# Preparing the second layer's weights for a fast pass: a second buffer for the high halves, low halves written over the sums, and decoding in four steps

## The chip, the cores and the metric

One core of one Trainium2 chip runs the whole program. The metric is the device time of one execution in microseconds. The kernel before took a median of 1413.3 us over three runs (1409.53, 1413.3 and 1413.33). A separate execution was recorded by the profiler; the rows below come from that one.

## The reference

Three layers follow each other, all in float32. The first is a linear attention with a decaying state for two sequences of 768 tokens; its output x has 1536 tokens of 512 values. The second is a mixture of eight experts whose gates are normalised in turn over experts and tokens. The third is a feed-forward layer with a leaky maximum:

```
for e in range(E):                      # 8 experts, F = 1024
    h = np.maximum(x @ w1[e], 0.0)
    ye = h @ w2[e]
    out += P[:, e:e + 1] * ye
...
h = x @ w_in                            # d_ff = 2048, two halves of 1024
g = np.maximum(h, 0.0) + alpha * np.minimum(h, 0.0)
return (g @ w_out).astype(np.float32)
```

The weights `w_in` and `w_out` arrive as 64-bit floating-point numbers, which the kernel turns into float32 itself.

## The kernel before

Every float32 product is made of three matmuls (`mm3`, lines 186 to 188): each operand is split into a high half (a rounded copy, made by ScalarE) and a low half (what is missing, made by a subtraction on VectorE or GpSimd).

The work runs in 20 phases of one sequence and one expert. Phases 0 to 7 are the eight experts for the first sequence, phases 8 to 15 the same experts for the second, and phases 16 to 19 the two halves of the feed-forward layer. A phase begins with 28 products, each of six matmuls (`product`), in the order of the list `order`: (0,1), (0,5), (0,6), (0,2), (0,7), (1,1), (1,5), (0,4), (1,6), (0,3), (1,2), (1,7), (2,1), (2,5), (1,4), (2,6), and so on; the first number is one of four blocks of the hidden layer, the second one of seven products from which a block is put together. After product (j,1) ScalarE copies bank A to bank B (line 686), and (j,6) adds to B. After (j,6) VectorE writes E from B (line 689), after (j,7) it writes D from B (line 702), and only then may (j,7) and (j,4) respectively add to B again. In phases 0 to 7 and 16 to 19 a second layer follows: six tiles of 128 tokens, each in two halves named t0a, t0, t1a, t1, ... t5a, t5, with 24 matmuls of 512 columns in a half.

In phases 8 to 15 the second layer, too, runs as a product scheme with fewer multiplications. It needs sums of the weights `w2`, which phases 1 to 7 prepare in 32 units. A unit loads a tile `pr` (line 158), forms four sums in it on VectorE (`prep_sums`, line 168), lets ScalarE write the high halves into a tile `pw` (line 170), writes the low halves into the same tile on VectorE (`prep_low`, line 177), and stores the 1 MB of `pw` to memory (`prep_store`, line 183). There is one buffer for `pw` and there are two for `pr`, so ScalarE's write for a unit waits until the store of the unit before it has landed.

The same phases decode the 64-bit weights in 32 steps: three operations on VectorE (`bits`), one on ScalarE (`power`), two more on VectorE (`join`), which also issues the store of 256 KB and the next load.

All this side work hangs on a table of hooks: `at(phase, key, functions)` puts functions behind a product or half tile. The order of the code is the order of each engine's queue, and an instruction that waits holds all that stand behind it on its engine. SyncE issues every transfer from one queue, in order. In phases 1 to 6 a unit's three steps stand at (0,2), (1,1), (1,6); at (2,5), (2,6), (2,7); and at t0a/t0/t1a, t2a/t2/t3a and t4a/t4/t5a. A decoding has all three steps at t1a, t3a and t5a, and stands ahead of the unit's store there.

Of the kernel before, what the change touches and what calls it, by code (L numbers as in the profile page):

```python
# [23 lines left out]
E, F = 8, 1024  # L24
# [5 lines left out]
NJ = NF // 2  # L30
TT = S // 128
# [13 lines left out]
def tile_kernel(ctx, tc, qkT, kv, ctab, w_gate, w1, w2, w_in, w_out, alpha, out):  # L45
    nc = tc.nc
# [7 lines left out]
    pools = {"raw1": stg}  # L54
# [19 lines left out]
    raw = {}  # L74
# [45 lines left out]
    def w1_part(n, part, eng):  # L120
        if n >= NJ * len(PHASES):
            return
        if part == "a":
            ws1[n] = {}
            if n < NJ * E:
                nc.sync.dma_start(out=c1[n], in_=raw[0, n][:, 768:1792])
# [27 lines left out]
    def prep_load(i):  # L154
        if i >= NJ * E:
            return
        pr[i] = tmp.tile([128, 1024], F32, tag=("ua", "ub")[i % 2], name=f"pr{i}")
        nc.sync.dma_start(out=pr[i], in_=w2[i])

    def prep_sums(i):  # L160
        s11, s21, s12, s22 = (pr[i][:, 256 * q:256 * q + 256] for q in range(4))
        for out, in0, in1, op in (
            (s22, s21, s22, ALU.add),
            (s21, s11, s21, ALU.subtract),
            (s11, s22, s11, ALU.subtract),
            (s12, s12, s11, ALU.subtract),
        ):
            nc.vector.tensor_tensor(out=out, in0=in0, in1=in1, op=op)  # L168
        ph2[i] = pools["prep"].tile([128, 4, 2, 256], F32R, tag="pw", name=f"pw{i}")
        nc.scalar.activation(  # L170
            out=ph2[i][:, :, 0, :], in_=pr[i].rearrange("p (a b) -> p a b", a=4), func=AF.Copy
        )

    def prep_low(i):
        v = pr[i].rearrange("p (a b) -> p a b", a=4)
        for a in (0, 2):
            nc.vector.tensor_tensor(  # L177
                out=ph2[i][:, a:a + 2, 1, :], in0=v[:, a:a + 2], in1=ph2[i][:, a:a + 2, 0, :].bitcast(F32),
                op=ALU.subtract,
            )  # L180

    def prep_store(i):
        nc.sync.dma_start(out=c2[i // NJ][:, i % NJ, 3:7], in_=ph2[i].bitcast(F32))

    def mm3(ps, ah, alo, bh, bl, first, last):
        nc.tensor.matmul(ps, ah, bh, start=first, stop=False, skip_group_check=True)  # L186
# [95 lines left out]
    with tc.manual_schedule():  # L282
# [293 lines left out]
        def decode_steps(u, then):  # L576
            kind, j, half = u
            held = {}

            def bits():  # L580
                t = held["t"] = rd.pop(u)
                lo, hi = (t.rearrange("p (f w) -> p f w", w=2)[:, :, q] for q in range(2))
                ex = held["ex"] = tp.tile([128, 512], U32, tag="tmp", name=f"ex{kind}_{j}_{half}")
                nc.vector.tensor_scalar(out=ex, in0=hi, scalar1=0x7FF00000, scalar2=None, op0=ALU.bitwise_and)  # L584
                a = held["a"] = tp.tile([128, 512], U32, tag="tmp", name=f"a{kind}_{j}_{half}")
                nc.vector.tensor_scalar(
                    out=a, in0=hi, scalar1=0x000FFFFF, scalar2=0x00100000, op0=ALU.bitwise_and, op1=ALU.bitwise_or
                )
                nc.vector.scalar_tensor_tensor(
                    out=a.bitcast(F32), in0=lo, scalar=2.0 ** -32, in1=a, op0=ALU.mult, op1=ALU.add  # L590
                )

            def power():
                nc.scalar.activation(out=held["ex"], in_=held["ex"], func=AF.Relu, bias=ebias, scale=8.0)  # L594

            def join():
                t, a, ex = (held[q] for q in ("t", "a", "ex"))
                hi = t.rearrange("p (f w) -> p f w", w=2)[:, :, 1]
                q = a.bitcast(F32)
                nc.vector.scalar_tensor_tensor(  # L600
                    out=q, in0=q, scalar=2.0 ** -20, in1=ex.bitcast(F32), op0=ALU.mult, op1=ALU.mult
                )
# [3 lines left out]
                nc.sync.dma_start(out=wd[kind][j][:, 512 * half:512 * half + 512], in_=q)  # L606
                if then:
                    decode_load(then)

            return bits, power, join  # L610


        banks, hq, late = {}, {}, []
# [268 lines left out]
        def at(ph, key, *fns):  # L882
            hooks.setdefault((ph, key), []).extend(fns)
# [18 lines left out]
        def prep_at(ph, k1, k2, k3):  # L902
            i = unit[0]
            if i >= NJ * E:
                return
            unit[0] += 1
            at(ph, k1, lambda: prep_load(i + 1), lambda: prep_sums(i))
            at(ph, k2, lambda: prep_low(i))
            at(ph, k3, lambda: prep_store(i))

        xk = []
        for ph in range(len(PHASES)):
# [23 lines left out]
                    at(ph, k1, lambda m=m: w1_adds(m, dve), lambda m=m: w1_part(m, "a", dve))  # L936
                    at(ph, k2, lambda m=m: w1_part(m, "c", dve), lambda m=m: w1_part(m, "b", dve))
            if 1 <= ph <= 6:
                for t in (1, 3, 5):
                    decode_at(ph, f"t{t}a", f"t{t}a", f"t{t}a")  # L940
                prep_at(ph, (0, 2), (1, 1), (1, 6))
                prep_at(ph, (2, 5), (2, 6), (2, 7))
                for t in (0, 2, 4):
                    prep_at(ph, f"t{t}a", f"t{t}", f"t{t + 1}a")
            elif ph == 7:
                prep_at(ph, (0, 2), (1, 1), (1, 6))
                prep_at(ph, (2, 5), (2, 6), (2, 7))
            elif fast:
                for q in ((6, 8, 9), (13, 15, 16)) if ph == E else ((4, 6, 7), (12, 14, 15)):
                    decode_at(ph, *(order[i] for i in q))  # L950
                if ph > E + 1:
                    for q in range(8):
                        at(ph, ((0, 5), (0, 7), (1, 5), (1, 6))[q // 2], lambda m=q // 2, h=q % 2: gather(m, h))
                at(ph, (0, 1), lambda ph=ph: weight_load(ph))
                for key, fn, jp in (
                    ((2, 2), t1, 0), ((3, 1), t2, 0), ((3, 6), t3, 0), ((3, 4), t1, 1), (1, t2, 1), (3, t3, 1),
                ):
                    at(ph, key, lambda ph=ph, fn=fn, jp=jp: fn(ph, jp))
                for k, key in enumerate(
                    ((1, 7), (3, 7), (2, 7), 0, (2, 4), 2, 4, 6, 8, 10, 12, 14, 16, 18)  # L960
                ):
                    at(ph, key, lambda ph=ph, k=k: hsplit(ph, k))
                for key, jp in ((5, 0), (7, 1)):
                    at(ph, key, lambda ph=ph, jp=jp: t4(ph, jp))
                if ph in (E + 1, E + 4):
                    at(ph, (0, 1), lambda k=(ph - E - 1) // 3: xk.extend(x_keep(2, k)))
                if E < ph < 2 * E - 1:
                    for keys in (((2, 1), (2, 2), (2, 7), (3, 4)), (9, 11, 13, 17), (18, 20, 22, 27)):
                        i = unit[0] - NJ * E
                        if i >= 7 * ((ph - E - 1) // 3 + 1):  # L970
                            continue
                        unit[0] += 1
                        for q, key in enumerate(keys):
                            at(ph, key, lambda i=i, q=q: xk[i][q]())
# [16 lines left out]
        for a, (key, later) in enumerate(zip(("t3", "t4", "t4", "t5"), (order[i] for i in (0, 1, 20, 22)))):  # L991
# [125 lines left out]
```

## Time and profile before

| quantity | value |
|---|---|
| median of three runs | 1413.3 us |
| profiled execution, its own time | 1405.09 us |
| profiled execution, span | 1403.4 us |
| TensorE busy | 1309.8 us (93%) |
| VectorE busy | 944.8 us (67%) |
| ScalarE busy | 633.9 us (45%) |
| GpSimd busy | 410.3 us (29%) |
| DMA engines, transfers of the hardware queue | 62.6% of their span |
| mean granted TensorE clock | 0.974 |

TensorE is the engine that is nearly always busy. Shares over the whole span hide that the phases differ, so the windows below follow phase boundaries: a phase begins where its first product does (phase 1 at 128.76 us, phase 2 at 197.93, phase 3 at 278.79, phase 7 at 593.09, phase 8 at 673.21). An idle time and its releaser stand in brackets behind the instruction that had to wait. "SPq" is SyncE's queue, "PEclk" the granted clock as a share of full speed.

### The profile page before, as it was taken

What the parts mean: (1) busy time and instruction counts of PE and PEld (TensorE: products, weight loads), DVE (VectorE), ACT (ScalarE), POOL (GpSimd) and SP (SyncE); (2) the same over time, 40 slices, a digit from 0 to 9 for tenths busy, and PEclk for the clock granted to TensorE, in tenths of its full rate; (3) what the DMA queues carried; (4) which work ended last, traced back from release to release, by engine and by line L of the source; (5) the groups of instructions that cost most, each with busy time, mean ns of one, the idle gap of its engine ahead of it and who ended that gap; (6) DMA issues with size and microseconds to landing.
All of it is one profiled execution on the core that took longest, in us unless ns stands there. A gap on an engine that the chain in (4) does not pass through costs nothing.

```text
span 1403.4 us, 19428 instructions
## 1 busy us (share of the span) xinstructions
PE 1309.8 (93%) x7179; PEld 1211.8 (86%) x7179; DVE 944.8 (67%) x1562; ACT 633.9 (45%) x1129; POOL 410.3 (29%) x335
## 2 busy tenths in 40 slices
PE   9899977979797988969999999999999999999998
PEld 6798867868676877868899999999999999889897
DVE  5656676767576676766576887877888576386462
ACT  2543525243332425244445464555645446465460
POOL 4751414131312314131000313123131335336250
PEclk9999999989899999989999999999999999999999
DMA  9563776859586777857776868768676393152201
GB/s 369 175 202 120 245 245 226 297 203 305 204 273 250 252 239 235 292 203 228 240 236 198 291 195 269 241 214 296 185 277 219 123 362 111 44 159 74 85 31 45
DMA packets 123070, 296.79 MB, mean 211 GB/s; under 512 B 11440, under 2 KB 43744, under 8 KB 118880
## 3 DMA queue, kind: packets, MB, share of 16 engines
q1 hardware_dynamic: 122976, 295.56, 62.6%
q8 instruction: 56, 0.92, 0.3%
q14 instruction: 38, 0.31, 0.1%
HBM read 198.24 MB, written 97.28 MB: 211 GB/s over the span
## 4 chain that ended last, share of the span: by engine, by line
PE 62%; DVE 13%; DMA 11%; ACT 6%; issue 4%; SPq 2%; POOL 1%; ACTq 0%; DVEq 0%
PE B L186 7%; DMA c<-pw 7%; PE B L188 7%; PE B L187 7%; PE o L186 5%; PE o L188 5%; PE o L187 5%; PE A L186 4%; PE A L187 4%; PE A L188 4%; DVE pw L177 3%; PE E L188 2%; PE E L186 2%; PE E L187 2%; PE D L188 2%
## 5 line engine op out<-in xcount | busy, mean ns | idle before, releaser
L113 POOL TENSOR_TENSOR raw<-raw 128x256 f32<-128x256 f32 x108 | 94.8, 888 | 234.9 <-DMA raw<-in_w_dram 73.7
L779 DVE TENSOR_TENSOR hs<-b,hs 128x768 fp32r<-128x768 f32 x96 | 97.4, 1015 | 30.9 <-ACT hs L778 30.9
L170 ACT ACTIVATE pw<-pr 128x1024 fp32r<-128x1024 f32 x32 | 33.9, 1059 | 173.7 <-DMA c<-pw 133.5
L778 ACT ACTIVATE hs<-b 128x768 fp32r<-128x768 f32 x96 | 81.1, 844 | 31.0 <-PE B L188 10.7
L811 POOL TENSOR_TENSOR total<-total,t 128x384 f32<-128x384 f32 x56 | 60.0, 1098 | 103.2 <-DVE t L807 103.2
L689 DVE TENSOR_TENSOR E<-B,d 128x384 f32<-128x384 f32 x80 | 45.1, 563 | 58.1 <-PE B L188 53.6
L686 ACT ACTIVATE B<-A 128x384 f32<-128x384 f32 x80 | 38.6, 482 | 87.8 <-PE A L188 86.2
L177 DVE TENSOR_TENSOR pw<-pr,pw 128x512 fp32r<-128x512 f32 x64 | 59.2, 967 | 25.8 <-ACT pw L170 25.8
L250 POOL TENSOR_TENSOR xs<-b,xs 128x384 fp32r<-128x384 f32 x6 | 9.3, 1548 | 193.4 <-ACT xs L246 193.4
L188 PE MATMUL B<-hs,ws 128*128 128x384 f32 x192 | 64.2, 334 | 0.0
L187 PE MATMUL B<-hs,ws 128*128 128x384 f32 x192 | 64.2, 334 | 0.0
L186 PE MATMUL B<-hs,ws 128*128 128x384 f32 x192 | 64.2, 334 | 0.0
L168 DVE TENSOR_TENSOR pr<-pr 128x256 f32<-128x256 f32 x128 | 55.2, 431 | 4.5 <-DMA pr<-in_w_dram 1.2
L594 ACT ACTIVATE ex<-ex,ebias 128x512 uint32<-128x512 uint32 x32 | 23.1, 721 | 63.1 <-DVE ex L584 63.1
L737 DVE SCALAR_TENSOR_TENSOR total<-o,P,total 128x512 f32<-128x512 f32 x42 | 31.3, 746 | 29.6 <-PE o L188 29.6
L702 DVE TENSOR_TENSOR D<-B,d 128x384 f32<-128x384 f32 x48 | 27.1, 565 | 31.4 <-PE B L188 31.0
L186 PE MATMUL A<-hs,ws 128*128 128x384 f32 x128 | 42.9, 335 | 0.0
L187 PE MATMUL A<-hs,ws 128*128 128x384 f32 x128 | 42.9, 335 | 0.0
L188 PE MATMUL A<-hs,ws 128*128 128x384 f32 x128 | 42.8, 335 | 0.0
L731 ACT ACTIVATE total<-o 128x512 f32<-128x512 f32 x18 | 10.8, 598 | 69.0 <-PE o L188 69.0
L113 DVE TENSOR_TENSOR raw<-raw 128x256 f32<-128x256 f32 x84 | 36.9, 457 | 1.4
L645 DVE SCALAR_TENSOR_TENSOR hl<-D,hh 128x384 fp32r<-128x384 f32 x32 | 17.8, 555 | 28.9 <-ACT hh L644 27.2
(3435 smaller groups left out, 4718.0 us busy)
## 6 DMA issues: line engine op xcount, KB each, us to landing
ws<-c SPq DMA_DIRECT2D x112, 512.0 KB, 5.5
raw<-in_w_dram SPq DMA_DIRECT2D x64, 512.0 KB, 4.9
c<-pw SPq DMA_DIRECT2D x32, 1024.0 KB, 6.7
c<-raw SPq DMA_DIRECT2D x32, 512.0 KB, 6.5
pr<-in_w_dram SPq DMA_DIRECT2D x32, 512.0 KB, 6.8
raw<-c SPq DMA_DIRECT2D x32, 512.0 KB, 5.9
raw<-wd SPq DMA_DIRECT2D x32, 512.0 KB, 3.6
raw<-in_w_dram SPq DMA_DIRECT2D x32, 384.0 KB, 4.8
```

The source lines that it names most:

```text
L113: eng.tensor_tensor(out=out, in0=in0, in1=in1, op=op)
L168: nc.vector.tensor_tensor(out=out, in0=in0, in1=in1, op=op)
L170: nc.scalar.activation(out=ph2[i][:, :, 0, :], in_=pr[i].rearrange("p (a b) -> p a b", a=4), func=AF.Copy)
L177: nc.vector.tensor_tensor(out=ph2[i][:, a:a + 2, 1, :], in0=v[:, a:a + 2], in1=ph2[i][:, a:a + 2, 0, :].bitcast(F32), op=ALU.subtract,)
L186: nc.tensor.matmul(ps, ah, bh, start=first, stop=False, skip_group_check=True)
L187: nc.tensor.matmul(ps, ah, bl, start=False, stop=False, skip_group_check=True)
L188: nc.tensor.matmul(ps, alo, bh, start=False, stop=last, skip_group_check=True)
L686: nc.scalar.activation(out=banks[n, "B"], in_=banks[n, "A"], func=AF.Copy)
L689: nc.vector.tensor_tensor(out=banks[n, "E"], in0=banks[n, "B"], in1=banks[n, "d"], op=add)
L778: nc.scalar.activation(out=hi, in_=src, func=AF.Copy)
L779: nc.vector.tensor_tensor(out=lo, in0=src, in1=hi.bitcast(F32), op=ALU.subtract)
L811: nc.gpsimd.tensor_tensor(out=dst, in0=dst, in1=tt[m, h], op=ALU.add)
```

## The change

Four things are edited. The high halves go to a tile `pw` of half the size with two buffers; the low halves are written over the sums in `pr`, which gets a third buffer; the store becomes two stores of 512 KB each, whose pieces in memory are 1 KB long where they were 8 KB. The decoding's store and next load are split off `join` as a fourth step. The hooks move: a decoding's steps spread over several half tiles, one decoding per phase goes into the products, and one unit of the preparation per phase goes from the products to the second layer. The store of the first layer's sums (`c1`) of two blocks per phase goes from part "a" to part "c". The space comes from a smaller scratch area that no transfer of this kernel uses.

```diff
-        pr[i] = tmp.tile([128, 1024], F32, tag=("ua", "ub")[i % 2], name=f"pr{i}")
+        pool = pools["prep"] if i % 3 == 2 else tmp
+        pr[i] = pool.tile([128, 1024], F32, tag="u" + "abc"[i % 3], name=f"pr{i}")
...
-        ph2[i] = pools["prep"].tile([128, 4, 2, 256], F32R, tag="pw", name=f"pw{i}")
-        nc.scalar.activation(
-            out=ph2[i][:, :, 0, :], in_=pr[i].rearrange("p (a b) -> p a b", a=4), func=AF.Copy
-        )
+        ph2[i] = pools["prep"].tile([128, 1024], F32R, tag="pw", bufs=2, name=f"pw{i}")
+        nc.scalar.activation(out=ph2[i], in_=pr[i], func=AF.Copy)
...
-        for a in (0, 2):
+        for a in (slice(0, 512), slice(512, 1024)):
             nc.vector.tensor_tensor(
-                out=ph2[i][:, a:a + 2, 1, :], in0=v[:, a:a + 2], in1=ph2[i][:, a:a + 2, 0, :].bitcast(F32),
-                op=ALU.subtract,
+                out=pr[i][:, a].bitcast(F32R), in0=pr[i][:, a], in1=ph2[i][:, a].bitcast(F32), op=ALU.subtract
             )
...
-        nc.sync.dma_start(out=c2[i // NJ][:, i % NJ, 3:7], in_=ph2[i].bitcast(F32))
+        for q, t in enumerate((ph2[i].bitcast(F32), pr[i])):
+            v = t.rearrange("p (a b) -> p a b", a=4)
+            nc.sync.dma_start(out=c2[i // NJ][:, i % NJ, 3:7, q, :], in_=v)
...
-            return bits, power, join
+            return bits, power, join, store
...
+        slots = [f"t{t}{w}" for t in range(TT) for w in ("a", "")]
...
-            at(ph, k2, lambda: prep_low(i))
+            hooks.setdefault((ph, k2), []).insert(0, lambda: prep_low(i))
...
-                for t in (1, 3, 5):
-                    decode_at(ph, f"t{t}a", f"t{t}a", f"t{t}a")
-                prep_at(ph, (0, 2), (1, 1), (1, 6))
-                prep_at(ph, (2, 5), (2, 6), (2, 7))
-                for t in (0, 2, 4):
-                    prep_at(ph, f"t{t}a", f"t{t}", f"t{t + 1}a")
+                if ph > 1:
+                    decode_at(ph, *(order[i] for i in (10, 12, 14, 18)))
+                for i in (2, 8):
+                    decode_at(ph, *(slots[i + q] for q in (0, 1, 2, (4, 3)[i > 2])))
+                prep_at(ph, order[8], order[10], order[12])
+                for i in (0, 3, 6, 9):
+                    prep_at(ph, *slots[i:i + 3])
```

In `order`, place 8 is (1,6), 10 is (1,2), 12 is (2,1), 14 is (1,4), 18 is (2,7) and 20 is (3,5). Phase 7 gets units at places 8, 10, 12 and 20, 22, 24 and one decoding at 10, 12, 14, 18. In the phases from 8 on the decodings' places move a little and get the fourth step; two transposes move in phase 8.

ScalarE, at the boundary of phases 2 and 3, before. `pw` are the high halves of a unit, `ex` a decoding, `B12` and `d12` the copies that the first products of phase 3 need:

```order
L170 ACTIVATE pw9_2814<-pr9_2715 128x4x256
L594 ACTIVATE ex0_2_1_2844<-ex0_2_1_2844,ebias_78 128x512
L686 ACTIVATE B12_2876<-A12_2869 128x384
L681 ACTIVATE d12_2889<-D12_2882 128x384
L644 ACTIVATE hh12_00_2905<-A12_2869 128x384
L97 ACTIVATE wa14h_2909<-raw0_14_2700 128x512
L170 ACTIVATE pw10_2919<-pr10_2808 128x4x256
L644 ACTIVATE hh12_11_2928<-D12_2882 128x384
```
The same place after the change:

```order
L171 ACTIVATE pw9_2831<-pr9_2758 128x1024
L687 ACTIVATE B12_2875<-A12_2868 128x384
L682 ACTIVATE d12_2888<-D12_2881 128x384
L645 ACTIVATE hh12_00_2904<-A12_2868 128x384
L97 ACTIVATE wa14h_2907<-raw0_14_2690 128x512
L645 ACTIVATE hh12_11_2918<-D12_2881 128x384
```
The decoding step between the last `pw` of phase 2 and the copy `B12` is gone, and so is the `pw` behind `wa14h`.

VectorE in the products of phase 3, from the E addition behind product (1,6) to the D addition behind (1,7), before:

```order
L689 TENSOR_TENSOR E13_2976<-B13_2943,d13_2959 128x384
L645 SCALAR_TENSOR_TENSOR hl12_10_2968<-B12_2876,hh12_10_2967 128x384
L645 SCALAR_TENSOR_TENSOR hl12_01_2987<-E12_2897,hh12_01_2986 128x384
L702 TENSOR_TENSOR D13_2952<-B13_2943,d13_2959 128x384
L645 SCALAR_TENSOR_TENSOR hl13_00_3002<-A13_2936,hh13_00_3001 128x384
```
The same place after:

```order
L690 TENSOR_TENSOR E13_2965<-B13_2934,d13_2948 128x384
L646 SCALAR_TENSOR_TENSOR hl12_10_2957<-B12_2875,hh12_10_2956 128x384
L169 TENSOR_TENSOR pr10_2825<-pr10_2825 128x256 x4
L646 SCALAR_TENSOR_TENSOR hl12_01_2983<-E12_2896,hh12_01_2982 128x384
L175 TENSOR_TENSOR pr10_2825<-pr10_2825,pw10_2974 128x512 x2
L583 TENSOR_SCALAR ex0_2_1_3007<-rd0_2_1_2864 128x512
L585 TENSOR_SCALAR a0_2_1_3009<-rd0_2_1_2864 128x512
L588 SCALAR_TENSOR_TENSOR a0_2_1_3009<-rd0_2_1_2864,a0_2_1_3009 128x512
L703 TENSOR_TENSOR D13_2941<-B13_2934,d13_2948 128x384
```
Between the two additions there now stand the sums (`pr10`) and low halves of a unit and the three operations of a decoding (`ex`, `a`).

SyncE at the end of phase 2's second layer, before. `wd` is the store of a decoding, `rd` the load of the next, `c2` the store of a unit, `raw` and `c1` belong to the first layer:

```order
L606 DMA wd0_2_124<-a0_2_0_2762 128x512
L574 DMA rd0_2_1_2769<-in_w_in_dram 128x1024
L183 DMA c2_2_114<-pw8_2721 128x2048
L91 DMA raw0_15_2793<-in_w1_dram 128x1024
L158 DMA pr10_2808<-in_w2_dram 128x1024
L606 DMA wd0_2_124<-a0_2_1_2846 128x512
L574 DMA rd0_3_0_2853<-in_w_in_dram 128x1024
L183 DMA c2_2_114<-pw9_2814 128x2048
```
The same place after:

```order
L182 DMA c2_2_114<-pw8_2764 128x4x256
L182 DMA c2_2_114<-pr8_2693 128x4x256
L159 DMA pr10_2825<-in_w2_dram 128x1024
L607 DMA wd0_2_124<-a0_2_0_2806 128x512
L573 DMA rd0_2_1_2864<-in_w_in_dram 128x1024
L182 DMA c2_2_114<-pw9_2831 128x4x256
L182 DMA c2_2_114<-pr9_2758 128x4x256
```
Before, each store of a unit stood behind the store of the decoding at its key; now the unit's two stores are ahead of the next decoding's store in one case and still behind one in the other.

## Rows read from the trace of the kernel before

**Rows 1.** Windows, one stretch a row, as its first line names them; (x) counts instructions.
```profile
core 0: us, PE busy (x) PEld busy (x) DVE busy (x) ACT busy (x) POOL busy (x), PEclk, DMA share, GB/s
128.70:197.90 69.20, 64.88 (x316) 58.02 (x316) 49.47 (x84) 31.17 (x54) 20.93 (x16) 0.98 0.72 243
197.90:593.10 395.20, 333.22 (x1562) 298.72 (x1561) 266.07 (x456) 142.20 (x240) 107.19 (x80) 0.93 0.74 250
278.80:357.30 78.50, 66.51 (x313) 59.65 (x312) 53.20 (x92) 28.45 (x48) 21.44 (x16) 0.93 0.74 250
593.10:673.20 80.10, 68.09 (x325) 60.99 (x324) 47.31 (x82) 33.03 (x61) 17.19 (x12) 0.94 0.65 223
1274.70:1337.00 62.30, 62.24 (x313) 56.08 (x312) 32.75 (x59) 31.52 (x57) 24.47 (x18) 1.00 0.23 73
```

**Rows 2.** Waits of TensorE: who waited, for whom, total us, times, longest.
```profile
PE B L186 <- ACT B L686: 53.6, 13, 7.1
```

**Rows 3.** Timeline of TensorE in phase 3: start, us, instruction, idle before and releaser.
```profile
285.80 0.69 PE L186 MATMUL B<-xh,wc12h 128*128 128x384 f32 x1 [4.77 <-ACT B L686]
...
289.00 0.34 PE L187 MATMUL A<-xl,wa12h 128*128 128x384 f32 x1
289.18 0.34 PE L188 MATMUL A<-xh,wa12l 128*128 128x384 f32 x1
...
297.43 0.69 PE L186 MATMUL B<-xh,wc13h 128*128 128x384 f32 x1 [3.75 <-ACT B L686]
...
311.28 0.44 PE L186 MATMUL B<-xh,wc14h 128*128 128x384 f32 x1 [0.87 <-DVE E L689]
...
317.29 0.44 PE L186 MATMUL B<-xh,wb14h 128*128 128x384 f32 x1 [2.60 <-DVE D L702]
```

**Rows 4.** Timeline of ScalarE at the start of phase 3.
```profile
281.84 1.06 ACT L170 ACTIVATE pw<-pr 128x1024 fp32r<-128x1024 f32 x1 [9.10 <-DMA c<-pw]
284.65 0.72 ACT L594 ACTIVATE ex<-ex,ebias 128x512 uint32<-128x512 uint32 x1 [1.76 <-DVE ex L584]
285.28 0.47 ACT L686 ACTIVATE B<-A 128x384 f32<-128x384 f32 x1
```

**Rows 5.** Timeline of SyncE's queue just before phase 3.
```profile
274.05 0.33 SPq L606 DMA_DIRECT2D wd<-a  x1
...
274.94 0.41 SPq L183 DMA_DIRECT2D c<-pw  x1
```

**Rows 6.** Timeline of VectorE in phase 3.
```profile
288.67 1.79 DVE L168 TENSOR_TENSOR pr<-pr 128x256 f32<-128x256 f32 x4
290.59 0.57 DVE L702 TENSOR_TENSOR D<-B,d 128x384 f32<-128x384 f32 x1
...
296.78 2.92 DVE L177 TENSOR_TENSOR pw<-pr,pw 128x512 fp32r<-128x512 f32 x2
...
333.21 1.29 DVE L177 TENSOR_TENSOR pw<-pr,pw 128x512 fp32r<-128x512 f32 x2
334.42 0.42 DVE L584 TENSOR_SCALAR ex<-rd 128x512 uint32<-128x512 uint32 x1
...
335.21 0.69 DVE L589 SCALAR_TENSOR_TENSOR a<-rd,a 128x512 f32<-128x512 uint32 x1
```

**Rows 7.** Timeline of GpSimd beside the row at 296.78.
```profile
297.08 2.07 POOL L98 TENSOR_TENSOR wc14l<-raw,wc14h 128x768 fp32r<-128x768 f32 x1 [5.14 <-ACT wc14h L97]
```

**Rows 8.** Windows: start of the second layer, all of it, the products, five us.
```profile
324.60:335.50 10.90, 10.90 (x50) 9.06 (x49) 7.78 (x18) 2.70 (x4) 1.16 (x1) 1.00 1.01 346
324.60:357.30 32.70, 32.70 (x146) 27.13 (x145) 25.77 (x48) 7.61 (x11) 5.32 (x5) 1.00 0.86 289
278.80:324.60 45.80, 33.81 (x169) 32.52 (x168) 27.43 (x45) 20.84 (x37) 16.12 (x12) 0.89 0.65 222
291.00:296.00 5.00, 2.68 (x16) 2.36 (x14) 0.61 (x2) 1.16 (x2) 0.94 (x1) 0.96 1.00 416
```

More of the change, by code (lines that the diff above doesn't have):

```diff
@@ L122, in w1_part @@
             return
+        if part == "ac"[n % NJ // 2] and n < NJ * E:
+            nc.sync.dma_start(out=c1[n], in_=raw[0, n][:, 768:1792])
         if part == "a":
             ws1[n] = {}
-            if n < NJ * E:
-                nc.sync.dma_start(out=c1[n], in_=raw[0, n][:, 768:1792])
             src, width, pieces = raw[0, n][:, 0:512], 512, (A11, A12)
@@ L168, in prep_sums @@
             nc.vector.tensor_tensor(out=out, in0=in0, in1=in1, op=op)
-        ph2[i] = pools["prep"].tile([128, 4, 2, 256], F32R, tag="pw", name=f"pw{i}")
-        nc.scalar.activation(
-            out=ph2[i][:, :, 0, :], in_=pr[i].rearrange("p (a b) -> p a b", a=4), func=AF.Copy
-        )
+        ph2[i] = pools["prep"].tile([128, 1024], F32R, tag="pw", bufs=2, name=f"pw{i}")
+        nc.scalar.activation(out=ph2[i], in_=pr[i], func=AF.Copy)
     def prep_low(i):
-        v = pr[i].rearrange("p (a b) -> p a b", a=4)
-        for a in (0, 2):
+        for a in (slice(0, 512), slice(512, 1024)):
             nc.vector.tensor_tensor(
-                out=ph2[i][:, a:a + 2, 1, :], in0=v[:, a:a + 2], in1=ph2[i][:, a:a + 2, 0, :].bitcast(F32),
-                op=ALU.subtract,
+                out=pr[i][:, a].bitcast(F32R), in0=pr[i][:, a], in1=ph2[i][:, a].bitcast(F32), op=ALU.subtract
             )
     def prep_store(i):
-        nc.sync.dma_start(out=c2[i // NJ][:, i % NJ, 3:7], in_=ph2[i].bitcast(F32))
+        for q, t in enumerate((ph2[i].bitcast(F32), pr[i])):
+            v = t.rearrange("p (a b) -> p a b", a=4)
+            nc.sync.dma_start(out=c2[i // NJ][:, i % NJ, 3:7, q, :], in_=v)
     def mm3(ps, ah, alo, bh, bl, first, last):
@@ L605, in join, with store @@
                 )
-                nc.sync.dma_start(out=wd[kind][j][:, 512 * half:512 * half + 512], in_=q)
+            def store():
+                nc.sync.dma_start(out=wd[kind][j][:, 512 * half:512 * half + 512], in_=held["a"].bitcast(F32))
                 if then:
                     decode_load(then)
-            return bits, power, join
+            return bits, power, join, store
         banks, hq, late = {}, {}, []
@@ L938, in tile_kernel @@
             if 1 <= ph <= 6:
-                for t in (1, 3, 5):
-                    decode_at(ph, f"t{t}a", f"t{t}a", f"t{t}a")
-                prep_at(ph, (0, 2), (1, 1), (1, 6))
-                prep_at(ph, (2, 5), (2, 6), (2, 7))
-                for t in (0, 2, 4):
-                    prep_at(ph, f"t{t}a", f"t{t}", f"t{t + 1}a")
+                if ph > 1:
[5 more added lines that the diff above has]
+                    prep_at(ph, *slots[i:i + 3])
             elif ph == 7:
-                prep_at(ph, (0, 2), (1, 1), (1, 6))
-                prep_at(ph, (2, 5), (2, 6), (2, 7))
+                decode_at(ph, *(order[i] for i in (10, 12, 14, 18)))
+                prep_at(ph, order[8], order[10], order[12])
+                prep_at(ph, order[20], order[22], order[24])
             elif fast:
-                for q in ((6, 8, 9), (13, 15, 16)) if ph == E else ((4, 6, 7), (12, 14, 15)):
+                for q in ((6, 8, 9, 11), (20, 22, 23, 25)) if ph == E else ((4, 6, 7, 8), (15, 17, 19, 21)):
                     decode_at(ph, *(order[i] for i in q))
@@ L990, in tile_kernel @@
             at(E, ((0, 7), (1, 5), (1, 6), (1, 2), (2, 1), (2, 6))[w], lambda w=w: ws_load(E, w))
-        for a, (key, later) in enumerate(zip(("t3", "t4", "t4", "t5"), (order[i] for i in (0, 1, 20, 22)))):
+        for a, (key, later) in enumerate(zip(("t3", "t4", "t4", "t5"), (order[i] for i in (0, 1, 14, 16)))):
             at(E - 1, key, lambda a=a: turn(2, a, 0))
@@ L1101 @@
     }
-    nc = bacc.Bacc("TRN2", target_bir_lowering=False, num_devices=1, dynamic_dma_scratch_size=1024)
+    nc = bacc.Bacc("TRN2", target_bir_lowering=False, num_devices=1, dynamic_dma_scratch_size=64)
     arrays, args = {}, []
```

## The prediction

> **What bounds the kernel now.** I read the windows by phase first. Phase 18, which prepares nothing, takes 62.3 us, and TensorE is busy in 62.24 of them; phases 2 to 6 take 395.2 us together, 79.0 each, with a granted clock of 0.93 where phase 18 has 1.00 [rows 1]. So some 16.7 us of each of these phases is not matmul work. The loss is not spread evenly. Phase 3 has a second layer of 32.7 us in which TensorE is busy throughout, and products of 45.8 us with 33.81 busy [rows 8]. At full rate the products would take 62.3 - 32.7 = 29.6 us, so the whole loss of 16.2 us stands in the products.
>
> The list of waits names the releaser: TensorE waits 53.6 us in all for ScalarE's copy of A to B [rows 2]. The timeline places it: 4.77 us before product (0,6) and 3.75 before (1,6), then two waits for VectorE, 0.87 and 2.60 [rows 3], together 11.99 us. After the first gap the ten matmuls from 285.80 to 289.00 come 0.32 us apart, while the next pair stands 0.18 apart [rows 3]: TensorE restarts at the lower of its two clock levels (1.2 GHz, not 2.4), which costs 10 x (0.32 - 0.18) = 1.4 us there. The second gap, and what the rounding of these rows hides, leaves 16.2 - 12.0 - 1.4 = 2.8 us, which I take as the same restart after the second gap.
>
> Why is the copy late? ScalarE's `pw` started at 281.84 after 9.10 us of waiting for the store of the unit before, a decoding step came behind it at 284.65, and the copy at 285.28 [rows 4]. That store was issued at 274.94, behind a decoding store at 274.05 [rows 5], and took 281.84 - 274.94 = 6.9 us to land. So the chain is: decoding on VectorE, SyncE's in-order queue, the store, the one `pw` buffer, ScalarE's queue, TensorE.
>
> **What the change removes.** With two buffers a `pw` waits for the store of two units earlier. In the second layer a unit comes every three half tiles, 3 x 32.7 / 12 = 8.2 us. A store follows its `pw` by two half tiles (5.5 us), and the buffer is wanted again 16.4 us after that `pw`: 10.9 us for a store of 6.9. Even with a few us of delay in SyncE's queue this holds. The decoding between the last `pw` and the copy is gone, too, and the second unit in the products, whose sums stood before the E addition and whose low halves stood before the D addition at the waits of 0.87 and 2.60. So all four waits and both restarts go: 16.2 us in phase 3, 16.7 in the mean of five phases.
>
> **What it adds, and what is late next.** Four terms per phase.
>
> First, VectorE's queue in the second layer. It works 25.77 us there now [rows 8]. The change puts in one more set of sums (1.79) and two more sets of low halves that now fall outside (2 x 1.29) [rows 6], while a decoding that ran over into the products goes to the products: 25.8 + 1.8 + 2.6 = 30.1 of 32.7 us. It also waits for ScalarE, since low halves now stand right behind their sums at two of four units and each `pw` takes 1.06 [rows 4], and it starts idle until the first tile is done (half a tile pair, 2.7 us, less the sums that fit in it). I put the end of its queue at 36.5 us from the layer's start. The E addition is wanted three products in, after 32.7 + 4 x 1.05 = 36.9 us, by TensorE's product (0,7); it takes about 0.57 like the D addition [rows 6]. So the wait is between 0 (the queue ends in time) and 3 us (GpSimd holds up VectorE); I take 1.0.
>
> Second, the D addition of block 1. Behind the E addition VectorE now has the sums, 1.79; then a low half of block 0 whose high half stands behind the unit's `pw` on ScalarE, 1.06 + 0.47 of idling; that low half, 0.5; the unit's low halves, 1.29 when free and 2.92 beside GpSimd; and a decoding's three operations, 0.42 + 0.42 + 0.69, or near double [rows 4, 6, 7]. With the E addition done 0.9 us after product (1,6), and one more low half of 0.5, the D addition ends after 0.9 + 0.5 + 1.8 + 1.5 + 0.5 + (1.3 to 2.9) + (1.5 to 2.9) + 0.6 = 8.6 to 11.6 us. TensorE wants it at product (1,4), five products or 5.2 us after (1,6). The wait is 3.4 to 6.4 us; I take 4.4, nearer the lower end, because GpSimd is busy in only 16.12 of 45.8 us of the products [rows 8], though it splits `w1` just there.
>
> Third, a restart at the lower clock after that wait, 1.4 to 2.8 us by the two of before: 2.0. Fourth, the E addition of block 2 follows late, behind a split of `w2` and the decoding's second half: 0 to 1.5, I take 0.5. Sum: 1.0 + 4.4 + 2.0 + 0.5 = 7.9 us, a phase of 62.3 + 7.9 = 70.2.
>
> On the low halves the trace shows 1.29 us for a pair at 333.21 and 2.92 for a pair at 296.78, while GpSimd's split ran from 297.08 to 299.15 [rows 6, 7]: the pair ended about half a microsecond after GpSimd did. The Trainium skill (SBUF — State Buffer, "Who interferes with whom") says that a VectorE tensor_tensor with both inputs in SBUF contends with GpSimd's reads, and that whoever issues second fully blocks. The trace agrees. It speaks against this change, which puts such operations on the way to a D addition; what it does if every one of them is caught is the slower rival below.
>
> The transfers move the same bytes. One more unit's load and store and one decoding less fall in the second layer, where the DMA share is 0.86 of 32.7 us [rows 8]. The 1 KB pieces cost something: in the stretch where the low and high halves of `w2` leave in such pieces, a share of 1.01 moved 346 GB/s, against 416 at 1.00 elsewhere [rows 8]. For 5 MB a phase that is 5243 x (1/346 - 1/416) = 2.5 us of DMA time, hidden unless the engines are full. The Trainium skill (DMA: Bandwidth & Descriptors, "Specifications") gives 512 B as the least transfer at line rate, by which these pieces would cost nothing; the row differs, and I go by the row. The forecast would be the same by either.
>
> **Sum.** Phases 2 to 6: 395.2 - 5 x 70.2 = 44.2 us. Phase 7 takes 80.1 [rows 1] and gains like them, less about 1 for its second unit in the products: 7. Phase 1 (69.2, so 6.9 above phase 18) loses small waits and gets the same sums before a D addition without a decoding: 1.5. The phases from 8 on keep their work: 0, give or take 2. Together 52.7 us, from the profiled 1405.1 to 1352.4. The median shown is 0.6% above the profiled execution and the fastest run 0.3%; between them I forecast 1355 us.
>
> **Rivals.** (A) VectorE keeps up: the D addition comes within the slack of two products, and the phases fall to 63.5. Then phases 2 to 6 give 395.2 - 317.5 = 77.7, phase 7 16, phase 1 5: 1306, some 1310 in the runs. For it: VectorE works 27.43 of 45.8 us in the products now [rows 8], and no row shows the new queue. Against it: the sum of the second term is above its slack at both ends.
>
> (B) The transfers become the bound of the second layer: 0.86 x 32.7 = 28.1 us of DMA time, plus a load and about 1.5 MB of stores at 416 GB/s (2.1 MB in 5.0 us), plus 2.5 for the short pieces, 35.6 against 32.7. Loads of `pr` come late, VectorE waits, and E is late by about 3 us more, with a second restart of about 2: 75 us a phase, a gain of 20 + 4, so 1381. Against it: phases have stretches of 0.65 in their products [rows 8] into which stores can slip.
>
> (C) Slower: GpSimd and VectorE block each other at every step. If each of the two low halves and three decoding operations waits out a GpSimd instruction (2.07 in rows 7, 1.3 for the shorter ones), the second term becomes about 10 us, the first about 6, and with two restarts of 2.8 and the 0.5 the sum is 22: a phase of 84, and 5 x 5 + 5 = 30 us more than before, 1436. It decides from a sum of 16.7 on, which is what is removed. Against it: GpSimd is idle in most of the stretch.
>
> (D) The change doesn't free ScalarE: stores are held in SyncE's queue behind a first-layer store or a decoding store so long that two buffers fill as well, and `pw` still waits: 1405 to 1413.
>
> **How the numbers follow.** Forecast 0.52, A 0.22, B 0.14, C 0.06, D 0.06. A measurement of this kernel tells a change of 0.3%, some 4 us, from none. The forecast, A and B are all faster, and of D a third: 0.90; D gives half of 0.06 to no change, 0.03; C and the rest of D 0.07. The forecast's own range, from its terms at both ends (sums of 4.8 to 13.7), is 1337 to 1382; taking in most of A and B, the range is 1318 to 1390.
>
> **What would show it.** Right: no wait of ScalarE's `pw` for a store, no wait of TensorE for the copy B, one wait per phase of 3 to 6 us before product (1,4) for D, a granted clock near 0.96 in phases 2 to 6. Wrong: no such wait (A), VectorE's sums waiting for `pr` and a DMA share near 1 in the second layer (B), low halves and decoding at twice their time throughout (C), or `pw` still released by a store (D).

## The result, and the profile after

The changed kernel took a median of 1389.6 us (1388.6 to 1390.6, four runs) against 1411.4 of the kernel before on the same chips: a ratio of 0.985 with an interval of 0.982 to 0.988. It is faster by 1.5%, some 22 us, where 58 were forecast (from 1413 to 1355). The time lies just inside the upper end of the stated range, 1318 to 1390. The two executions whose profiles are compared below lie closer together than the medians: their spans are 1403.4 and 1388.9 us, 14.5 apart.

The windows follow the phases again. The first row is phases 2 to 6 together, the second phase 3, then phases 7, 8, and 9 to 15. The columns are those of [rows 1].

```profile
197.64:570.15 372.51, 329.24 (x1562) 295.06 (x1560) 267.89 (x455) 143.24 (x240) 105.76 (x80) 0.94 0.80 265
272.94:347.90 74.96, 66.48 (x314) 59.39 (x313) 54.77 (x93) 29.13 (x49) 21.14 (x16) 0.93 0.81 267
570.15:649.61 79.46, 67.56 (x325) 59.95 (x324) 53.36 (x90) 33.85 (x62) 17.99 (x12) 0.94 0.70 234
649.61:714.66 65.05, 61.91 (x351) 61.13 (x350) 44.28 (x64) 32.86 (x57) 0.00 (x0) 0.97 0.72 234
714.66:1132.90 418.24, 410.18 (x2353) 407.97 (x2353) 319.27 (x438) 220.39 (x376) 94.11 (x83) 1.00 0.71 233
```

Phases 2 to 6 fell from 395.2 to 372.5 us, 74.5 each, where 70.2 were forecast. Phase 7 went only from 80.1 to 79.5. The later phases lost time. Here are phases 8 and 9 to 15 of the kernel before:

```profile
673.20:736.50 63.30, 60.63 (x351) 59.56 (x350) 44.39 (x64) 32.67 (x57) 0.00 (x0) 1.00 0.73 242
736.50:1149.00 412.50, 410.34 (x2353) 407.94 (x2353) 319.30 (x438) 221.48 (x376) 94.97 (x83) 1.00 0.71 236
```

So phase 8 is 1.75 us longer, at a granted clock of 0.97 instead of 1.00, and phases 9 to 15 are 5.7 us longer, 7.5 together. The work of phases 9 to 15 is the same in both: 2353 matmuls and 438 VectorE instructions. What grew there is TensorE's wait for the E addition. In this list for the changed kernel's phases 9 to 15 it is the only wait (the kernel before has 1.5 us of it, and 0.7 for another operation):

```profile
PE B L185 <- DVE E L690: 8.1, 6, 1.6
```

Over the whole execution, TensorE's waits (who waited, for whom, total us, times, longest) answer to [rows 2]:

```profile
PE B L185 <- DVE D L703: 40.3, 8, 5.8
PE B L185 <- ACT B L687: 16.3, 7, 3.8
PE B L185 <- DVE E L690: 13.3, 10, 3.1
```

The wait for the copy B fell from 53.6 to 16.3 us; a wait for the D addition has taken its place. The timeline of TensorE in phase 3 answers to [rows 3]:

```profile
277.57 0.44 PE L185 MATMUL B<-xh,wc12h 128*128 128x384 f32 x1 [2.38 <-ACT B L687]
...
298.01 0.69 PE L185 MATMUL B<-xh,wb13h 128*128 128x384 f32 x1 [5.82 <-DVE D L703]
...
302.65 0.34 PE L187 MATMUL E<-xh,wb13l 128*128 128x384 f32 x1
```

`wb13h` at 298.01 is the product (1,4), the place that the prediction named. The 14 steps from there to the matmul at 302.65 are nearly all 0.32 us long, the lower clock level. They take 4.64 us, against 14 x 0.175 = 2.45 at full rate, so 2.2 us more are lost.

VectorE's and GpSimd's timelines show why D is late. VectorE answers to [rows 6], GpSimd to [rows 7]:

```profile
287.08 0.57 DVE L690 TENSOR_TENSOR E<-B,d 128x384 f32<-128x384 f32 x1 [2.53 <-PE B L187]
...
288.02 2.62 DVE L169 TENSOR_TENSOR pr<-pr 128x256 f32<-128x256 f32 x4
292.19 0.56 DVE L646 SCALAR_TENSOR_TENSOR hl<-E,hh 128x384 fp32r<-128x384 f32 x1 [1.55 <-ACT hh L645]
292.67 2.35 DVE L175 TENSOR_TENSOR pr<-pr,pw 128x512 fp32r<-128x512 f32 x2
294.94 1.48 DVE L583 TENSOR_SCALAR ex<-rd 128x512 uint32<-128x512 uint32 x1
296.34 0.41 DVE L585 TENSOR_SCALAR a<-rd 128x512 uint32<-128x512 uint32 x1
296.79 0.69 DVE L588 SCALAR_TENSOR_TENSOR a<-rd,a 128x512 f32<-128x512 uint32 x1
297.40 0.56 DVE L703 TENSOR_TENSOR D<-B,d 128x384 f32<-128x384 f32 x1
```
```profile
286.57 3.33 POOL L113 TENSOR_TENSOR raw<-raw 128x256 f32<-128x256 f32 x4
292.76 1.72 POOL L98 TENSOR_TENSOR wb14l<-raw,wb14h 128x512 fp32r<-128x512 f32 x1 [2.85 <-ACT wb14h L97]
294.43 1.71 POOL L98 TENSOR_TENSOR wa15l<-raw,wa15h 128x512 fp32r<-128x512 f32 x1
```

The queue is what the order of the change says: sums, idling for the high half behind `pw` (1.55), low halves, three decoding operations, then D at last, which starts 10.3 us after the E addition did. Three of these took longer than in [rows 6]: the sums, which ran beside GpSimd's additions, 2.62 us instead of 1.79; the low halves, beside its two splits, 2.35 instead of 1.29; and the decoding's first operation, beside the second split, 1.48 instead of 0.42.

The wait for the copy B has another cause than before. First VectorE, then ScalarE with the list of what `pw` waits for, then SyncE, with what its queue waited for between 256 and 266 us:

```profile
272.14 0.43 DVE L583 TENSOR_SCALAR ex<-rd 128x512 uint32<-128x512 uint32 x1 [2.63 <-DMA rd<-in_w_in_dram]
```
```profile
ACT pw L171 <- DVE pr L169: 136.0, 30, 8.9
276.09 1.06 ACT L171 ACTIVATE pw<-pr 128x1024 fp32r<-128x1024 f32 x1 [2.70 <-DVE pr L169]
277.05 0.47 ACT L687 ACTIVATE B<-A 128x384 f32<-128x384 f32 x1
```
```profile
SPq L124 <- DVE raw L113: 4.8, 1, 4.8
261.76 0.33 SPq L124 DMA_DIRECT2D c<-raw  x1
262.19 0.38 SPq L182 DMA_DIRECT2D c<-pw  x1
262.62 0.91 SPq L182 DMA_DIRECT2D c<-pr  x1
263.57 1.30 SPq L607 DMA_DIRECT2D wd<-a  x1
264.92 1.19 SPq L573 DMA_DIRECT2D rd<-in_w_in_dram  x1
```

No store of a unit holds `pw` any more, where [rows 4] showed 9.10 us for one. Of its 32 waits 30 are for the sums; the other two, 2.3 and 2.6 us, are put down to a store, but end within 0.1 us of the sums. But the load `rd` for the second layer's second decoding stands in SyncE's queue behind a first-layer store, two stores of a unit and a decoding store. The first of these waited 4.8 us for VectorE's additions and held the others. The load is issued at 264.92, VectorE waits 2.63 us for it, and behind it stand the last unit's sums, its `pw`, and the copy B.

### The profile page after: what moved, and what is told of

It reads as the page before. It is cut to its first block, busy times and chain, and to the rows that moved or that the text cites. A ratio compares the mean times of both kernels' runs of the same rounds, so it can differ in the third digit from the quotient of the medians.

```text
span 1388.9 us, 19473 instructions
## 1 busy us (share of the span) xinstructions
PE 1306.0 (94%) x7179; PEld 1208.2 (87%) x7179; DVE 946.9 (68%) x1562; ACT 634.6 (46%) x1129; POOL 408.6 (29%) x335
## 3 DMA queue, kind: packets, MB, share of 16 engines
q1 hardware_dynamic: 152160, 295.57, 64.2%
## 4 chain that ended last, share of the span: by engine, by line
PE 66%; DVE 18%; ACT 6%; DMA 5%; issue 3%; SPq 2%; POOL 1%; ACTq 0%; DVEq 0%
PE B L185 8%; PE B L187 7%; PE B L186 7%; PE o L185 5%; PE o L187 5%; PE o L186 5%; PE A L185 4%; PE A L187 4%; PE A L186 4%; DVE pr L169 3%; DVE pr L175 3%; PE E L185 2%; PE E L186 2%; PE E L187 2%; PE D L187 2%
## 5 line engine op out<-in xcount | busy, mean ns | idle before, releaser
L113 POOL TENSOR_TENSOR raw<-raw 128x256 f32<-128x256 f32 x108 | 90.1, 845 | 207.3 <-DMA raw<-in_w_dram 62.5
L169 DVE TENSOR_TENSOR pr<-pr 128x256 f32<-128x256 f32 x128 | 65.8, 514 | 3.3
L249 POOL TENSOR_TENSOR xs<-b,xs 128x384 fp32r<-128x384 f32 x6 | 6.1, 1022 | 199.8 <-ACT xs L245 199.8
L187 PE MATMUL B<-hs,ws 128*128 128x384 f32 x192 | 64.2, 334 | 0.0
L185 PE MATMUL B<-hs,ws 128*128 128x384 f32 x192 | 64.2, 334 | 0.0
L186 PE MATMUL B<-hs,ws 128*128 128x384 f32 x192 | 64.2, 334 | 0.0
L175 DVE TENSOR_TENSOR pr<-pr,pw 128x512 fp32r<-128x512 f32 x64 | 48.7, 803 | 16.9 <-ACT pw L171 16.9
L113 DVE TENSOR_TENSOR raw<-raw 128x256 f32<-128x256 f32 x84 | 42.2, 519 | 1.4
L645 ACT ACTIVATE hh<-D 128x384 fp32r<-128x384 f32 x32 | 15.7, 490 | 49.3 <-DVE D L703 49.3
L682 ACT ACTIVATE d<-D 128x384 f32<-128x384 f32 x64 | 31.1, 486 | 15.0 <-PE D L187 14.9
```

What stands on the lines that cost most here:

```text
L113: eng.tensor_tensor(out=out, in0=in0, in1=in1, op=op)
L175: nc.vector.tensor_tensor(out=pr[i][:, a].bitcast(F32R), in0=pr[i][:, a], in1=ph2[i][:, a].bitcast(F32), op=ALU.subtract)
L186: nc.tensor.matmul(ps, ah, bl, start=False, stop=False, skip_group_check=True)
L187: nc.tensor.matmul(ps, alo, bh, start=False, stop=last, skip_group_check=True)
```

## The experiments

The reasons under test: theory Q says the change lost its gain in VectorE's queue, by where it puts the unit and the decoding; theory T says the transfers, in shorter pieces and with late loads, took it. The first four kernels ran on one chip, the other four later on another. Ratios are against the kernel before on the same chip; its medians on the two, 1411.4 and 1413.0 us, differ by 0.1%.

**The storage alone.** The change's two `pw` buffers, three `pr` buffers and two stores, with all hooks (and the store of `c1`) at the places of before.

```diff
-                prep_at(ph, order[8], order[10], order[12])
-                for i in (0, 3, 6, 9):
-                    prep_at(ph, *slots[i:i + 3])
+                for t in (1, 3, 5):
+                    decode_at(ph, f"t{t}a", f"t{t}a", f"t{t}a", f"t{t}a")
+                prep_at(ph, (0, 2), (1, 1), (1, 6))
+                prep_at(ph, (2, 5), (2, 6), (2, 7))
+                for t in (0, 2, 4):
+                    prep_at(ph, f"t{t}a", f"t{t}", f"t{t + 1}a")
...
```

> The storage of the change (two buffers for pw, three for pr, two stores per unit) with the places of the kernel before. Theory Q (VectorE's queue between the E and the D addition, and its late end in the second layer, are what the change lost): the waits for a store go, and no unit with a decoding stands between the E and D addition of block 1; phases 2 to 6 look like phase 1 of the kernel before (69.2 us), 69 to 71 us each, so 1355 to 1370 us, faster than the change by 20 us or more. Rival T (the transfers, with 1 KB pieces and late loads, are what the change lost): phases stay at 74 to 76 us, 1385 to 1395 us.

Measured: 1342.2 us, ratio 0.950 (0.946 to 0.953), better than either theory said. The window is phases 2 to 6:

```profile
197.16:536.07 338.91, 318.46 (x1562) 286.43 (x1560) 273.31 (x456) 143.59 (x241) 105.70 (x80) 0.98 0.88 291
```

That is 67.8 us a phase, with the short pieces and a DMA share of 0.88. One half of theory T falls here: the same short stores at a higher rate (291 GB/s against 265) cost nothing that shows. Its other half, late loads, is not tested by this kernel, since the loads, too, stand at the places of before. The storage is worth 69 us; with it in place, the new places give 47 of them back.

**The places alone.** The storage functions of before in the change.

```diff
-        ph2[i] = pools["prep"].tile([128, 1024], F32R, tag="pw", bufs=2, name=f"pw{i}")
+        ph2[i] = pools["prep"].tile([128, 4, 2, 256], F32R, tag="pw", name=f"pw{i}")
...
```

> The places of the change with the storage of the kernel before (one pw buffer of 1 MB, one store of 8 KB pieces per unit). Both theories: a unit every 8.2 us with a store that is issued 5.5 us after its pw and lands 6.9 us later makes ScalarE wait some 4 us per unit in the second layer; the waits of ScalarE for a store come back, over 80 us in all. Theory Q: the waits for the D addition stay as well, so it is slower than the kernel before, 1415 to 1450 us. Rival T: without the short pieces the loads come in time, so it is between the two, 1390 to 1410 us.

Measured: 1413.2 us, ratio 1.0005 (0.999 to 1.002): no change, a little under Q's interval and above T's. So with the old storage the places cost some 2 us, not clear of noise, against 47 with the new: the effects of storage and places don't add up. ScalarE waits for stores as expected, and TensorE for D as in the change:

```profile
ACT pw L170 <- DMA c<-pw: 119.1, 15, 12.5
```
```profile
PE B L186 <- DVE D L704: 40.3, 8, 5.8
```

The wait for D is 40.3 us with the old storage, too, the same as with the new: it belongs to the places.

**The later phases' places.** The change with the decodings and transposes of phases 8 to 15 where they were.

```diff
-                for q in ((6, 8, 9, 11), (20, 22, 23, 25)) if ph == E else ((4, 6, 7, 8), (15, 17, 19, 21)):
+                for q in ((6, 8, 9, 9), (13, 15, 16, 16)) if ph == E else ((4, 6, 7, 7), (12, 14, 15, 15)):
...
```

> The change with the decodings and transposes of phases 8 to 15 at the places of the kernel before. Theory Q: phases 8 to 15 go back from 483.3 us to 475.8, the waits for the E addition of block 3 there vanish; 1381 to 1384 us. Rival (these phases are slower because of traffic left over from phase 7, or scatter between executions): no change, 1387 to 1391 us.

Measured: 1384.9 us, ratio 0.980 (0.975 to 0.985). Its four executions scatter from 1379.5 to 1391.7 us, so the time alone does not tell this kernel from the change (1388.6 to 1390.6); the phases do. Phases 8 and 9 to 15, and the wait for E in the latter:

```profile
651.15:717.00 65.85, 63.16 (x351) 62.31 (x350) 44.37 (x64) 33.07 (x57) 0.00 (x0) 0.95 0.71 229
717.00:1131.06 414.06, 410.55 (x2354) 407.88 (x2353) 320.00 (x438) 221.25 (x376) 94.95 (x83) 1.00 0.71 236
```
```profile
PE B L185 <- DVE E L690: 2.5, 5, 0.8
```

Phases 9 to 15 get 4.2 of their 5.7 us back, and the wait for E falls from 8.1 to 2.5. The whole set of kernels bears this out: the six with the change's places there take 418.2 to 418.3 us for these phases, the four with the places of before 412.5 to 414.2. Phase 8 gets nothing back, so its 1.75 us are not explained by its decodings and transposes. It has a granted clock of 0.95 here, lower still than the 0.97 of the change.

**The load earlier.** The first decoding of the second layer issues its store and next load with the join, ahead of the first-layer store.

```diff
-                    decode_at(ph, *(slots[i + q] for q in (0, 1, 2, (4, 3)[i > 2])))
+                    decode_at(ph, *(slots[i + q] for q in (0, 1, 2, (2, 3)[i > 2])))
```

> The change with the store and next load of the second layer's first decoding one step earlier, at t2a with the join, ahead of the first layer's store in SyncE's queue. Theory L (the 2.63 us that VectorE waits for the decoding's load at t4a makes the sums and pw of the last unit late, and so the copy B): the wait for the load falls under 0.5 us, the wait of TensorE for the copy falls from some 2.4 us to under 1 in phases 2 to 6, 8 to 14 us less in all, 1375 to 1382 us. Rival W (VectorE has too much work there anyway, 30 of 32.7 us): the copy is as late as before, 1387 to 1391 us.

Measured: 1371.0 us, ratio 0.970 (0.966 to 0.975), a little more than expected; phases 2 to 6 take 71.7 us each. In phase 2 the load now goes out ahead of the first-layer store, and VectorE's operation on it no longer waits:

```profile
254.80 0.43 SPq L573 DMA_DIRECT2D rd<-in_w_in_dram  x1
...
264.74 0.42 DVE L583 TENSOR_SCALAR ex<-rd 128x512 uint32<-128x512 uint32 x1
```

TensorE's list of waits no longer has the copy B; what it has is the D addition, 40.3 us as before, and some more for E:

```profile
PE B L185 <- DVE E L690: 18.3, 14, 3.1
```

So rival W falls, and the late loads of theory T are shown to cost something, by their place in the queue. This one place was worth 19 us: 2.8 us in each of phases 2 to 6, and in phase 7 the 79.5 became 76.0. The next three kernels keep this edit, to take the wait for D apart.

**The decoding behind D.**

```diff
-                    decode_at(ph, *(order[i] for i in (10, 12, 14, 18)))
+                    decode_at(ph, *(order[i] for i in (18, 20, 22, 24)))
```

> As the run with the early load, and the decoding in the products moved from places 10, 12, 14, 18 to 18, 20, 22, 24. Theory Q (the D addition of block 1 is late by just what stands ahead of it on VectorE): the three decoding operations (1.48 + 0.41 + 0.69 less overlaps, 2.5 us) leave the stretch, the wait for D falls from 5.83 to about 3.3 us in phases 2 to 7, each phase gets 2.5 to 4 us shorter, 1348 to 1358 us. Rival (ScalarE's pw and the high half behind it set the D addition, or the decoding costs the same at its new place): the wait stays above 5 us, or the phases stay at 71.7; 1367 to 1374 us.

Measured: 1360.1 us, ratio 0.964 (0.961 to 0.967). The wait in phase 3:

```profile
285.02 0.69 PE L185 MATMUL B<-xh,wb13h 128*128 128x384 f32 x1 [3.36 <-DVE D L703]
```

3.36 for 3.3 expected, and 69.5 us a phase, but 2 us more in all than the range said: phase 7 keeps its decoding there, and with it its wait of 5.83.

**The low halves behind D.**

```diff
-                prep_at(ph, order[8], order[10], order[12])
+                prep_at(ph, order[8], order[12], order[14])
```

> As the run with the early load, and the low halves of the unit in the products moved behind the D addition, from place 10 to 12, with the stores at 14; sums and pw stay. Theory Q: 2.3 us of low halves leave the stretch, the wait for D falls from 5.83 to about 3.5 us, 1350 to 1360 us. Rival: no change, 1367 to 1374 us.

Measured: 1364.0 us, ratio 0.966 (0.964 to 0.968), between the theory's range and the rival's. The wait fell only to 4.5 where 3.5 were expected. TensorE in phase 3, and VectorE, which shows why:

```profile
286.69 0.69 PE L185 MATMUL B<-xh,wb13h 128*128 128x384 f32 x1 [4.51 <-DVE D L703]
```
```profile
282.67 0.42 DVE L583 TENSOR_SCALAR ex<-rd 128x512 uint32<-128x512 uint32 x1
283.00 1.50 DVE L585 TENSOR_SCALAR a<-rd 128x512 uint32<-128x512 uint32 x1
284.53 1.63 DVE L588 SCALAR_TENSOR_TENSOR a<-rd,a 128x512 f32<-128x512 uint32 x1
```

The 2.35 us of low halves went and the first decoding operation is back at 0.42, but now the other two stand beside GpSimd's splits (282.75 to 285.61 us) and take 1.50 and 1.63 instead of 0.41 and 0.69. Whichever operation of VectorE's stands beside the splits is the one that takes longer.

**GpSimd out of the way.** GpSimd's splits of the first layer's weights behind D, in phases 2 to 7.

```diff
+                ka, kc, kb = ((j, 2), (j, 7), (j, 3)) if not 1 < ph < E else ((0, 2), (0, 7), (1, 4)) if j == 0 else ((1, 4), (2, 6), (1, 3))
...
```

> As the run with the early load, and GpSimd's splits of w1 (second part of the third block, all parts of the fourth) moved behind the D addition in phases 2 to 7, so that nothing of GpSimd's stands beside the unit's low halves and the decoding. Theory S (the low halves, 2.35 instead of 1.29 us, and the decoding's first operation, 1.48 instead of 0.42, were held up by GpSimd): both return to their free times and the wait for D falls by about 2.1 us to 3.7; 1352 to 1362 us. Rival (their length has another cause, the lower clock or ScalarE): durations and wait unchanged, 1367 to 1374 us.

Measured: 1368.4 us, ratio 0.969 (0.966 to 0.971): the durations and the wait as theory S expected, the time not. It lies in the rival's range. Its gain over the run with the early load is 0.2%, on another chip, and the kernel before differs by 0.1% between the two.

```profile
284.42 1.28 DVE L175 TENSOR_TENSOR pr<-pr,pw 128x512 fp32r<-128x512 f32 x2
285.62 0.42 DVE L583 TENSOR_SCALAR ex<-rd 128x512 uint32<-128x512 uint32 x1
```
```profile
287.63 0.45 PE L185 MATMUL B<-xh,wb13h 128*128 128x384 f32 x1 [3.69 <-DVE D L703]
```

Both operations are back at their free times and the wait is 3.69 for 3.7. Most of the 2.1 us went to new small waits: up to 0.4 us for GpSimd's `wc` split, up to 0.6 for the D addition of block 2 and 0.4 to 2.1 for the copy B. In phases 2 to 6 the gain is 0.6 us each.

**The storage with the second unit later.** The first kernel of this section with one more edit, in phases 1 to 7.

```diff
-                prep_at(ph, (2, 5), (2, 6), (2, 7))
+                prep_at(ph, order[20], order[22], order[24])
```

> As the run with the change's storage at the old places, and the second unit of the products at places 20, 22, 24 instead of (2,5), (2,6), (2,7). Theory Q: its sums no longer stand before the E addition of block 2 nor its low halves before the D addition, the waits of 2.16 and 1.0 to 2.6 us in phases 1 to 7 become at most the 0.9 and 1.4 that phase 7 of the change shows for these places; 64 to 66 us a phase, 1322 to 1334 us. Rival (the unit costs the same wherever it stands): 1339 to 1345 us.

Measured: 1322.3 us, ratio 0.937 (0.935 to 0.939). It beats both kernels, the changed one by 67 us.

```profile
195.50:521.49 325.99, 313.86 (x1561) 280.25 (x1560) 274.61 (x452) 143.62 (x240) 106.81 (x80) 1.00 0.90 301
```

65.2 us a phase, at full clock and with a DMA share of 0.90: the transfers still don't bound the phases. Phase 8 is as short here as in the kernel before, with the hooks that it has in the third kernel:

```profile
590.00:653.39 63.39, 60.64 (x351) 59.58 (x350) 44.39 (x64) 32.78 (x57) 0.00 (x0) 1.00 0.74 242
```

What sets phase 8's length apart is the clock. TensorE waits 2.3 to 3.1 us for the E addition there in every kernel. In five (the kernel before, the first, the fifth, the seventh and this one) the clock stays at 1.00 behind that wait and the phase takes 63.0 to 64.0 us; in the other five it falls to 0.95 to 0.97 and the phase takes 64.6 to 65.9. The first row is the wait in the change, followed by one of ten steps of 0.32 us; the second is the same wait in the fifth kernel (the decoding behind D), which has the same hooks in phase 8, no slow steps and 63.95 us:

```profile
680.70 0.44 PE L185 MATMUL B<-xh,wc35h 128*128 128x384 f32 x1 [3.08 <-DVE E L690]
...
682.16 0.52 PE L185 MATMUL E<-xh,wb35h 128*128 128x384 f32 x1
```
```profile
651.18 0.44 PE L185 MATMUL B<-xh,wc35h 128*128 128x384 f32 x1 [3.00 <-DVE E L690]
```

The ten steps cost 10 x (0.32 - 0.175) = 1.45 us, most of the 1.75 that phase 8 lost. Why the clock fell behind one of these waits and not behind the other stays open.

## Why the prediction was wrong

The direction, the wait for a store that would go and the wait for D that would come were right. But TensorE's wait for the copy B stayed, from a cause that the prediction had not looked for, and the kernel gained 22 us, less than half of the 58 forecast. Of the 38 us between the 52.7 forecast for the profiled execution and the 14.5 measured, 21.5 lie in phases 2 to 6, 6.3 in phase 7 and 7.5 in phases 8 to 15. By its steps:

*What is removed.* Right for the store: `pw` waits for no unit's store any more, and the storage alone shows what that is worth without the new places, 69 us. Wrong in saying that all four waits of [rows 3] go: the one for the copy B before product (0,6) is 2.38 us in phase 3, where it was 4.77. Two of the signs that the prediction named for being right failed with it: no wait for the copy B (16.3 us are left), and a granted clock near 0.96 in phases 2 to 6 (0.94).

*First term, the end of VectorE's queue in the second layer, taken as 1.0 us.* This is the step that failed most. It counted VectorE's work and ScalarE's copies, but not the decoding's load. The load stood behind a first-layer store in SyncE's queue; ahead of phases 2 to 6 it made VectorE wait 1.4 to 3.5 us, and at their start TensorE waited 1.2 to 3.4 us for the copy B, 0.1 to 0.3 less each time. With the load earlier TensorE waits 1.0 us for E, the term as written, and the run is 19 us faster. That the number fits is partly luck: 1.0 was picked between 0 and 3, while the working before it (36.5 + 0.57 against 36.9) gives 0.2. The prediction did list SyncE's queue under (D), for stores only.

*Second term, the D addition, taken as 4.4 us in a range of 3.4 to 6.4.* Right in kind and place, but too small; it measured 5.83. I took the value near the lower end because GpSimd is busy in a third of the products, an average. At this place it worked in 6.2 of the 10.3 us between the two additions, right beside VectorE's operations, and the run with GpSimd's splits later returned 2.1 of the 5.83. The sums, which I had at 1.79 in both bounds, took 2.62. The low halves, 2.35 us beside the splits and 1.28 without them, bear out the rule on two inputs in SBUF that the prediction quotes from the Trainium skill (SBUF — State Buffer, "Who interferes with whom"). That rule should have set the value. The decoding's first operation, which has one input, took longer too (1.48, and 0.42 without the splits); the rule as quoted does not speak of it.

These two terms account for phases 2 to 6: they take 74.5 us each instead of 70.2, 4.3 more, of which the early load gave back 2.8 and 5.83 - 4.4 = 1.4 is the second term's miss.

*Third term, the lower clock, 2.0 us.* Right for the wait that it was meant for, and one short. Phase 3 lost 74.96 - 62.3 = 12.7 us, of which 2.38 + 5.82 = 8.2 are the two waits of its rows. Of the other 4.5 the restart after the wait for D costs 2.2. Some 1.8 more go to a second stretch at the lower level, from 278.74 to 282.11 us, behind the wait for the copy B, which the sum did not have.

*Fourth term, E of block 2, 0.5.* Too large: 0.2 in one phase.

*Phase 7, forecast to gain 7.* It gained 0.7: it had the same late copy (3.76 us) and late D, and the waits of 0.9 and 1.4 for its second unit, which the forecast had at about 1 together.

*Phases from 8 on, 0 give or take 2.* Wrong: 7.5 us lost there. I did not walk their queues. 4.2 of them are shown to belong to the decodings' new places in phases 9 to 15. In phase 8 some 1.5 of the 1.75 are a stretch at the lower clock, whose coming or going the runs don't explain; the remaining 1.5 of phases 9 to 15 stay open.

*The last steps of the sum.* By the prediction's own percentages, 0.3 to 0.6% on 1352.4 give 1356 to 1360, not 1355. And the terms at their upper end, 13.7 instead of 7.9 in five phases, give some 1384 for 1355, not 1382. Neither changes the account.

The rival (B) gives a time near the measured one, 1381, but not by its mechanism: VectorE's sums waited for no load of `pr`, and the run with the highest DMA share (0.90) is the fastest. What (B) named rightly was a late load, and that came from its place in the queue: with the load earlier the wait is gone, at a DMA share of 0.84 in phases 2 to 6 against 0.80 in the change. The short pieces cost about what the prediction estimated: the hardware queue's share rose from 62.6% of 1403.4 us to 64.2% of 1388.9 for the same bytes, 13 us more or 1.9 in each of phases 1 to 7, where 2.5 were estimated. That traffic costs nothing at all is not shown, since no run took the stores away.

Outside the steps, the prediction weighed storage and places as one thing. The old places with the new storage, priced by themselves, would have shown two waits of 1.0 to 2.6 us in most phases (2.16 for E and 1.0 to 2.6 for D in the run with the storage alone) where the new places have one of 5.8.

## What to carry to other kernels

When a change frees a buffer and moves work as well, price the two apart and together: here the buffers alone were worth 69 us, and the moves cost 47 on top of them, but nothing clear without them. Before side work is put between two instructions that feed the critical engine, add up the queue there at the durations it has beside its neighbours at that very place, not at those of an average. And walk every in-order queue that a moved step passes, loads included: one load behind a store that waited for an engine cost 19 us.

## What the runs showed that was not expected

VectorE's four sums took longer beside GpSimd's additions, too: 2.62 us at 288.02 against 1.79 in [rows 6], while four additions ran on GpSimd from 286.57 to 289.90. No run moved these additions away, but in the changed kernel's trace every set of four sums with nothing of GpSimd's beside it takes 1.79 or 1.80. And TensorE does not always restart slowly at once after a wait: behind the one of 2.38 us at 277.57 the first matmuls came at full rate, and the slow ones only from 278.74 on:

```profile
278.37 0.35 PE L186 MATMUL B<-xl,wc12h 128*128 128x384 f32 x1
...
279.04 0.53 PE L186 MATMUL A<-xl,wa12h 128*128 128x384 f32 x1
279.36 0.53 PE L187 MATMUL A<-xh,wa12l 128*128 128x384 f32 x1
```
